# S3 from A11 and A21, two small products exchanged, sums of w_in stored on SP, and one set of q loads earlier, in a fused attention and feed-forward kernel

## The chip, the cores and the metric

The kernel runs on one core of a Trainium2 chip. The engines of the core work beside each other, each through its own instructions in program order: TensorE (PE) multiplies, VectorE (DVE) adds, subtracts and transposes, ScalarE (ACT) squares and copies, GpSimd (POOL) and SyncE (SP) issue transfers. The metric is the time of one execution on the device in microseconds (us), as the median of several; profiles come from one further execution.

## The reference

All tensors are float32. q, k and v have shape (8 batches, 8 heads, 576 rows, 64).

```
kv  = einsum("bhsd,bhse->bhde", k, v)
out = einsum("bhsd,bhde->bhse", q, kv)
x   = out / sqrt(mean(out*out, axis=-1) + 1e-6) * g_norm     # per head
x   = transpose(x, (0, 2, 1, 3)).reshape(4608, 512)
h   = x @ w_in                       # 512 x 2048
g   = s * relu(h)**2 + b
out = g @ w_out                      # 2048 x 512
```

The attention is small. Nearly all arithmetic is in the two products with w_in and w_out.

## The kernel before

The 4608 tokens are cut into nine units of 512, u = 0 to 8. For each, `mm1` computes h and the squared ReLU, and `mm2` computes the product with w_out. Both use Winograd's form of Strassen's scheme: a product of 2 by 2 blocks is made of seven block products instead of eight, for which sums of blocks are formed first: S1 = A21 + A22, S2 = S1 − A11, S3 = A11 − A21, S4 = A12 − S2 on the left, and T1 to T4 in the same way on the right. The seven products have the numbers 1 to 7 in the code: 1 is A11·B11, 2 is A12·B21, 3 is S4·B22, 4 is A22·T4, 5 is S1·T1, 6 is S2·T2, 7 is S3·T3.

Units 0 and 1 go one level deep. Units 2 to 8 are called deep here. In `mm1_deep`, products 2, 3 and 4 are split once more (`small(i, pair, *ms)`, with m the number of the inner product), in the order listed in `DEEP`. In `mm2`, function `rest()` does the same by groups of products: 1, then 2 and 5 together, 6, then 7 and 3 together, then 4. The line of nearly every matmul is that of a helper, L92; additions are L260, subtractions L263, and the fused addition with ReLU L267.

**The four slices of A.** The left operand of mm2, g, lies in tiles ga[name, s] for s = 0 to 3 with names a11, a12, a21, a22 and s1. VectorE writes S2 into the tile of A11, S4 into that of A12, and S3 into that of A21, each in its turn (`s1`, `s2`, `s3`, `s4`, one 128x512 instruction per slice). Before the change S3 is formed as A22 − S2, which is the same value, so it can only come once S2 stands in A11's tile; the four steps come in `rest()` right after S4, between `go_6(7)` and `do_6(5)`. ScalarE makes the square of each A block and applies s and b in `done(name, *slices)` (L944, L651).

**Sums and their buffers.** The sums of weights and of x for the inner products are made by VectorE in buffers with the tag "sub", of which there are six: `sums_of_w_in` (two parts for each of the five keys in `DEEP`), `parts_of_w` (sums of w_out; three with this tag, one with another), `sums_of_x`, `sums_of_x4`, and the quarter sums of mm2. A buffer is free once its last reader is done; for sums of weights that is the transfer that stores them to DRAM. `sums_of_w_in` is made in unit 1 and stored at L794 by POOL into `w1_dram`; `parts_of_w` is made in unit 1's mm2 and stored at L1143 by POOL into `w3_dram`.

**The ring.** From unit 1 on, weights and stored sums come from DRAM through a ring of 14 slots of 256 KB. SP issues the loads in the order of use (`queue_w2`); `used()` frees slots and `pump()` issues the next loads.

**The order of work.** The order on every engine is the order of the program: it is written out by hand in `run()` (mm1 of a deep unit, with `at(n)` for side work), in `rest()` (mm2) and in the tables of `sides()` and `side_of()`. The attention of a later unit is side work: `loads` (q, by `load_q`, L1653, 16 transfers of 32 KB on POOL for one half unit), `turn` (L540, transposes of q on VectorE), `product` (L552, TensorE), `back` (L564), `square`, `row_sum`, `norm`, `turn_x` and `scale`. Output stores (L1246) are on POOL too, until the last unit.

In unit 1, POOL's order around the change is as follows. In mm1: q loads, among which stand the ten stores of `sums_of_w_in`. In mm2: four stores of sums for key 5, four output stores, four stores for key 3, eight output stores, four stores for key 4, four output stores, and then sixteen q loads, `loads(3, 1)`, at step 13 of `side_of`.

Of the kernel before, what the change touches and what calls it, by code (L numbers as in the profile page):

```python
# [17 lines left out]
def kernel(  # L18
# [39 lines left out]
    nc = tc.nc  # L58
# [13 lines left out]
    NS = FC // 4  # L72
# [189 lines left out]
    def sub(o, a, b):  # L262
        nc.vector.tensor_tensor(out=o, in0=a, in1=b, op=ALU.subtract)  # L263
# [47 lines left out]

    w2_dram = [dram.tile([P, 2, FC // 2, P], FP32, name=f"w2_{i}") for i in range(8)]
    w3_dram = [dram.tile([P, 4, FC // 4, P], FP32, name=f"w3_{i}") for i in range(8)]
    DEEP = ((2, 0), (4, 0), (3, 0), (2, 1), (3, 1))
    w1_dram = {key: dram.tile([P, 2, 4 * P], FP32, name=f"w1_{key[0]}{key[1]}") for key in DEEP}
    w_up = convp.tile([P, FC // 2, DM], FP32, name="w_up")
    w_dn = convp.tile([P, FC // 2, DM], FP32, name="w_dn")
# [317 lines left out]
    ga, g_pair = {}, {}  # L635
# [143 lines left out]
    def sums_of_w_in(key):  # L779

        i, pair = key
        w = [
            ws[s][:, 2] if i == 3 else (wa if i == 2 else wb)[s][:, KH:]
            for s in (2 * pair, 2 * pair + 1)
        ]
        a11, a12, a21, a22 = w[0][:, 0], w[0][:, 1], w[1][:, 0], w[1][:, 1]
        t = {}

        def part(n, *steps):
            x = late["sub"].tile([P, FC // 4, P], FP32, name="sub", tag="sub", bufs=6)  # L790
            t[n] = x[:, :2], x[:, 2:]
            for step in steps:
                step()
            nc.gpsimd.dma_start(  # L794
                out=w1_dram[key][:, n], in_=x.rearrange("p f n -> p (f n)")
            )

        return (
            lambda: part(
                0,  # L800
                lambda: sub(t[0][1], a11, a21),
                lambda: sub(t[0][0], a22, t[0][1]),
            ),
            lambda: part(
                1,
                lambda: add(t[1][0], a21, a22),
                lambda: sub(t[1][1], a12, t[0][0]),
            ),
        )

    def mm1_deep(u):
# [54 lines left out]
        def a22(s):  # L866
            t = g_tile("a22", s)
            add_relu(t, st["y", s], ga["a21", s])
# [8 lines left out]
            g_s1(s)  # L877

        def s3(s):
            sub(ga["a21", s], ga["a22", s], ga["a11", s])  # L880

        def small(i, pair, *ms):
            name = {2: "a11", 3: "a21", 4: "a12"}[i]
            g = (i, pair)
            apart = g == (3, 0)

            def to(j, h):
                return g_pair[name, pair][:, j, :, h * P : h * P + P]

            def w_of(m):  # L890
                s0, s1 = 2 * pair, 2 * pair + 1
                raw = {1: (s0, 0), 2: (s0, 1), 4: (s1, 1)}
                if m in raw:
                    s, k = raw[m]
                    return ws[s][:, 2, k] if i == 3 else (wa if i == 2 else wb)[s][:, KH + k]
                n, k = {6: (6, 0), 7: (6, 1), 5: (5, 0), 3: (5, 1)}[m]
                return ring[u, g, n][:, k]

            def bank_for(m):
                if apart:  # L900
                    ps = ps_t.tile([P, 2, 2 * P], FP32, name="st_ps", tag="t")
                    return ps[:, 0].rearrange("p (b c) -> p b c", c=P)
                if m == 1:
                    ps = ps_a.tile([P, DM], FP32, name="sx_ps", tag="x")
                    return ps.rearrange("p (b c) -> p b c", c=P)[:, :2]
                ps = bank_of(("s", m), "z", 1).rearrange("p b (m c) -> p (b m) c", c=P)
                return ps[:, :2]

            def keep(n, j, h):
                tag = f"q{n}" if apart else {1: "r14", 2: "r2_2", 4: "q4"}[n]  # L910
                if apart:
                    tag += "t"
                st[g, n] = late["tmp"].tile([P, 2, P], FP32, name="r", tag=tag)
                add(st[g, n], st[g, "x"], to(j, h))

            for m in ms:
                first = m in (1, 2, 7)
                if first:
                    st[g, "x" if m == 1 else "y"] = bank_for(m)
                ps = st[g, "x" if m in (1, 6, 5, 3) else "y"]  # L920
                w, x = w_of(m), a[i, m]
                for b in range(2):
                    matmul(ps[:, b], w[:, b], x, first and b == 0, True)
                if m == 7:
                    used((u, g, 6))
                elif m == 3:
                    used((u, g, 5))
                if m == 1:
                    keep(1, 0, 0)
                elif m == 2:  # L930
                    add_relu(to(0, 0), ps, st[g, 1])
                elif m == 6:
                    keep(2, 1, 0)
                elif m == 5:
                    keep(4, 1, 1)
                    add_relu(to(1, 1), st[g, "y"], st[g, 4])
                elif m == 3:
                    add_relu(to(0, 1), ps, to(0, 1))
                elif m == 4:
                    add_relu(to(1, 0), ps, st[g, 2])  # L940

        def done(name, *steps):
            for s in steps:
                nc.scalar.square(ga[name, s], ga[name, s])  # L944
                affine(ga[name, s])

        def run(at, early):
            x1(0)
            at(2)
            x1(1)  # L950
            sums_of_x()
            small(2, 0, 1, 2)
            x6(0)
            at(4)
            at(5)
            small(2, 0, 6, 7)
            y7(0)
            at(6)
            small(2, 0, 5)
            a12(0)  # L960
            x6(1)
            at(7)
            small(2, 0, 3, 4)
            y7(1)
            sums_of_x4()
            a12(1)
            x5(0)
            small(4, 0, 1, 2)
            a22(0)
            done("a11", 0, 1)  # L970
            at(8)
            x5(1)
            small(4, 0, 6, 7)
            at(9)
            a22(1)
            done("a22", 0)
            at(10)
            x1(2)
            at(11)
            small(4, 0, 5)  # L980
            x1(3)
            at(12)
            small(4, 0, 3, 4)
            done("a22", 1)
            x6(2)
            at(13)
            small(3, 0, 1, 2)
            y7(2)
            done("a12", 0, 1)
            at(14)  # L990
            small(3, 0, 6, 7)
            small(2, 1, 1, 2)
            x6(3)
            at(15)
            small(3, 0, 5)
            small(2, 1, 6, 7)
            x5(2)
            small(3, 0, 3, 4)
            small(2, 1, 5)
            a22(2)  # L1000
            y7(3)
            done("a21", 0, 1)
            small(2, 1, 3, 4)
            at(16)
            x5(3)
            done("a22", 2)
            s1(0)
            s1(1)
            done("a11", 2, 3)
            a22(3)  # L1010
            early()
            at(18)
            y4(2)
            done("a22", 3)
            small(3, 1, 1, 2)
            done("a12", 2)
            y4(3)
            small(3, 1, 6, 7)
            done("a12", 3)

        def rest_of_3():
# [2 lines left out]

        last = dict(
            p3_5=lambda: small(3, 1, 5), p3_34=rest_of_3,
            s1=lambda: (s1(2), s1(3)), s3=lambda: [s3(s) for s in range(NS)],
        )
        return run, last

# [70 lines left out]
    def mm2(u, step=None, side={}):  # L1101
# [301 lines left out]
        def rest():  # L1403
# [18 lines left out]
            do_1(4)  # L1422
            do_25(2)
            at(1)
            s2((0,))
            do_25(6)
            s2((1,))
# [16 lines left out]
            do_6(2, 6)  # L1444
            s4((1, 2, 3))
            go_6(7)
            step["s3"]()
            do_6(5)
            sums_73((5, 6), 7)
            sums_73((), 3)  # L1450
# [175 lines left out]
    def side_of(A, B, sums, u):  # L1626

        if u == 0:
            return {
                6: [A["turn"], lambda: kv_product(1)],  # L1630
                8: [A["product"], A["back"], A["square"]],
                9: [A["row_sum"], B["turn"]],
                10: [A["norm"], partial(loads, 2, 0), A["turn_x"], A["scale"], B["product"], B["back"], B["square"]],
                11: [B["row_sum"], B["norm"]],
                12: [B["turn_x"], B["scale"], lambda: [fn() for fn in sums_w_in(0)]],
                13: [sums],
            }
        return {
            0: [A["scale"]],
            1: [B["turn"]],  # L1640
            4: [B["product"], B["back"], B["square"]],
            5: [B["row_sum"]],
            6: [B["norm"]],
            8: [B["turn_x"], B["scale"]],
            11: [sums],
            13: [partial(loads, 3, 1)],
        }

    def loads(u, i):
# [131 lines left out]
    for u in range(U):  # L1781
# [16 lines left out]
        for s in range(NS if u > 0 else 0):  # L1798
            a = steps[s]

            def at(n):
                for fn in first.get((s, n), []):
                    fn()
# [75 lines left out]
```

## Time and profile before

| | us |
|---|---|
| median of three executions | 919.71 (919.36 to 922.05) |
| the profiled execution | 921.89 |
| its span in the profile | 920.1 |

| engine | busy us | share |
|---|---|---|
| PE | 897.6 | 98% |
| DVE | 684.2 | 74% |
| ACT | 345.2 | 38% |
| POOL | 266.6 | 29% |

A line of the timeline has the start and length in us, the engine, the line in the kernel, the operation, what is written and read by the program's names, its size, and the number of instructions put together. In brackets stand the idle time of the engine just before it and what ended that. A line of the waits names the engine, what waited, what it waited for, and then the total in us, the times, and the longest. In the page's list of groups the busy time comes first and then the mean length of one in ns.

### The profile page before, as it was taken

What the parts mean: (1) busy time and instruction counts of PE and PEld (TensorE: products, weight loads), DVE (VectorE), ACT (ScalarE), POOL (GpSimd) and SP (SyncE); (2) the same over time, 40 slices, a digit from 0 to 9 for tenths busy, and PEclk for the clock granted to TensorE, in tenths of its full rate; (3) what the DMA queues carried; (4) which work ended last, traced back from release to release, by engine and by line L of the source; (5) the groups of instructions that cost most, each with busy time, mean ns of one, the idle gap of its engine ahead of it and who ended that gap; (6) DMA issues with size and microseconds to landing.
All of it is one profiled execution on the core that took longest, in us unless ns stands there. A gap on an engine that the chain in (4) does not pass through costs nothing.

```text
span 920.1 us, 19738 instructions
## 1 busy us (share of the span) xinstructions
PE 897.6 (98%) x7662; PEld 827.2 (90%) x7662; DVE 684.2 (74%) x1321; ACT 345.2 (38%) x584; POOL 266.6 (29%) x503
## 2 busy tenths in 40 slices
PE   7999999999999999999999999999999999999998
PEld 6888888888879998999899989999999989999998
DVE  2898687785467977688768876887769786974686
ACT  3887024422157005620464026601660066104610
POOL 2037066223721334701570037303520300021000
PEclk9999999999999999999999999999999999999999
DMA  9898647459833985388636973587539812982185
GB/s 255 315 320 244 172 121 252 146 151 350 298 102 108 310 291 159 87 285 287 192 95 212 292 258 77 170 291 264 135 112 293 276 47 65 299 293 66 60 277 180
DMA packets 121166, 188.77 MB, mean 205 GB/s; under 512 B 25457, under 2 KB 43249, under 8 KB 121073
## 3 DMA queue, kind: packets, MB, share of 16 engines
q1 hardware_dynamic: 100304, 159.03, 54.2%
q0 software_dynamic: 17312, 26.25, 9.5%
q10 hardware_dynamic: 3456, 2.23, 1.0%
q8 instruction: 61, 1.00, 0.4%
q14 instruction: 33, 0.26, 0.1%
HBM read 160.70 MB, written 26.74 MB: 204 GB/s over the span
## 4 chain that ended last, share of the span: by engine, by line
PE 81%; DVE 13%; DMA 4%; ACT 1%; issue 1%; ACTq 0%; DVEq 0%; SPq 0%; POOLq 0%
PE x_ps L92 39%; PE y_ps L92 22%; PE z_ps L92 8%; PE sx_ps L92 5%; DVE a L263 4%; PE st_ps L92 2%; DVE sub L263 2%; DVE o L260 2%; PE y_ps L552 2%; DMA w_sb<-w 1%; DVE sub L260 1%; DMA kv_sb<-in_v_dram 1%; DVE r L260 1%; PE kv_ps L384 1%; PE z_ps L384 1%
## 5 line engine op out<-in xcount | busy, mean ns | idle before, releaser
L1653 POOL DMA_DIRECT2D q_sb<-in_q_dram x312 | 175.4, 570 | 120.2 <-issue 61.6
L1246 POOL DMA_DIRECT2D out_dram<-o x120 | 59.4, 502 | 341.5 <-issue 174.5
L92 PE MATMUL x_ps<-w_sb,sub 128*128 128x128 f32 x1176 | 149.2, 276 | 0.1
L92 PEld LDWEIGHTS x_ps<-w_sb,sub 128*128 128x128 f32 x1176 | 139.7, 192 | 0.3 <-DVE r L260 0.2
L651 ACT ACTIVATE a<-a,b_col,s_col 128x512 f32<-128x512 f32 x144 | 117.0, 814 | 27.8 <-DVE a L654 19.5
L848 ACT COPY a<-x_ps 128x512 f32<-128x512 f32 x28 | 16.3, 582 | 246.7 <-PE x_ps L92 246.6
L92 PE MATMUL y_ps<-xs,wb 128*128 128x256 f32 x416 | 98.5, 380 | 0.0
L92 PE MATMUL x_ps<-xs,ws_raw 128*128 128x256 f32 x384 | 91.2, 380 | 1.3 <-ACT r L725 1.3
L92 PE MATMUL x_ps<-xT,wa 128*128 128x256 f32 x360 | 85.8, 387 | 0.1
L92 PEld LDWEIGHTS y_ps<-xs,wb 128*128 128x128 f32 x416 | 76.3, 190 | 9.1 <-issue 0.2
L92 PEld LDWEIGHTS x_ps<-xs,ws_raw 128*128 128x128 f32 x384 | 70.0, 190 | 10.3 <-ACT r L725 2.1
L92 PEld LDWEIGHTS x_ps<-xT,wa 128*128 128x128 f32 x360 | 67.6, 193 | 11.1 <-ACT a L944 1.3
L92 PE MATMUL x_ps<-w_sb,a 128*128 128x128 f32 (+1 forms) x432 | 66.4, 301 | 7.6 <-issue 7.6
L944 ACT ACTIVATE a<-a 128x512 f32<-128x512 f32 x112 | 69.5, 621 | 5.5 <-DVE a L267 5.5
L92 PEld LDWEIGHTS x_ps<-w_sb,a 128*128 128x128 f32 x432 | 58.9, 191 | 12.1 <-issue 9.1
L260 DVE TENSOR_TENSOR r<-sx_ps,a 128x256 f32<-128x256 f32 x84 | 35.0, 417 | 41.3 <-PE sx_ps L92 40.9
L92 PE MATMUL y_ps<-w_sb,a 128*128 128x128 f32 (+1 forms) x416 | 62.1, 295 | 0.0
L92 PEld LDWEIGHTS y_ps<-w_sb,a 128*128 128x128 f32 x416 | 56.1, 192 | 2.1
L260 DVE TENSOR_TENSOR r<-x_ps,o 128x256 f32<-128x256 f32 (+1 forms) x84 | 29.6, 352 | 31.9 <-PE x_ps L92 29.4
L92 PE MATMUL y_ps<-w_sb,sub 128*128 128x128 f32 x392 | 50.2, 277 | 1.4 <-DVE sub L263 1.4
L92 PEld LDWEIGHTS y_ps<-w_sb,sub 128*128 128x128 f32 x392 | 46.5, 192 | 2.7 <-DVE sub L263 2.7
L92 PE MATMUL z_ps<-w_sb,a 128*128 128x128 f32 (+1 forms) x352 | 46.9, 280 | 0.0
(228 smaller groups left out, 1595.0 us busy)
## 6 DMA issues: line engine op xcount, KB each, us to landing
w_sb<-w SPq DMA_DIRECT2D x413, 256.0 KB, 4.6
w<-sub POOLq DMA_DIRECT2D x38, 256.0 KB, 4.9
w_sb<-w SPq DMA_DIRECT2D x14, 512.0 KB, 8.7
out_dram<-o POOLq DMA_DIRECT2D x112, 64.0 KB, 4.0
w_sb<-in_k_dram SPq DMA_DIRECT2D x24, 288.0 KB, 4.2
w_sb<-in_v_dram SPq DMA_DIRECT2D x24, 288.0 KB, 4.4
w_raw<-in_moe_w_in_dram SPq DMA_DIRECT2D x6, 1024.0 KB, 8.0
q_sb<-in_q_dram POOLq DMA_DIRECT2D x160, 32.0 KB, 3.4
```

What stands on the lines that cost most here:

```text
L92: nc.tensor.matmul(o, lhsT=lhsT, rhs=rhs, start=start, stop=stop, skip_group_check=True)
L260: nc.vector.tensor_tensor(out=o, in0=a, in1=b, op=ALU.add)
L263: nc.vector.tensor_tensor(out=o, in0=a, in1=b, op=ALU.subtract)
L384: nc.tensor.matmul(ps[r][(r ^ l) * HB : (r ^ l) * HB + HB, i, :], lhsT=kv[l][0][rows, j, :], rhs=kv[l][1][rows, j, :], start=(j == 0), sto ...
L552: nc.tensor.matmul(ps[l][32 * p : 32 * p + 32, r, lo:hi], lhsT=bd_kv[b % 2][rows, p, at : at + 32], rhs=st["qT"][rows, p, lo:hi], start=Tr ...
L651: nc.scalar.activation(t, t, AF.Identity, scale=s_col, bias=b_col)
L848: nc.scalar.copy(g_tile("a11", s), st["x", s])
L944: nc.scalar.square(ga[name, s], ga[name, s])
L1246: queues[s % 2].dma_start(out=view[b, jj, :, cols], in_=st[name, j][s * w : s * w + w, cols])
L1653: load()
```

## The change

It has four parts.

1. S3 is computed as A11 − A21, in place in A21's tile, and therefore before S2 overwrites A11. Slices 0 and 1 move into `run()`, slices 2 and 3 into `rest()` ahead of the first S2. S1 of slices 0 and 1 also moves to earlier places in `run()`.
2. In `run()`, the small products of S4·B22 (key (3, 0)) and of A22·T4 (key (4, 0)) exchange places, with the keys in `DEEP`, the squares of A21 and A12 (`done`), and the choice of which of the two uses banks of its own (`apart`). `sums_of_x4` and A22 of slice 1 move as well.
3. The ten stores of `sums_of_w_in` are issued by SP instead of POOL.
4. `loads(3, 1)`, q for the second half of the unit with u = 3, is issued at step 9 of unit 1's mm2 instead of step 13: on POOL it now stands behind the stores of key 5 and ahead of the output stores that follow them.

No matmul, addition or activation is added or removed.

```diff
-    DEEP = ((2, 0), (4, 0), (3, 0), (2, 1), (3, 1))
+    DEEP = ((2, 0), (3, 0), (4, 0), (2, 1), (3, 1))
...
-            nc.gpsimd.dma_start(
+            nc.sync.dma_start(
                 out=w1_dram[key][:, n], in_=x.rearrange("p f n -> p (f n)")
             )
...
         def s3(s):
-            sub(ga["a21", s], ga["a22", s], ga["a11", s])
+            sub(ga["a21", s], ga["a11", s], ga["a21", s])
...
-            apart = g == (3, 0)
+            apart = g == (4, 0)
...
             small(2, 0, 3, 4)
             y7(1)
-            sums_of_x4()
             a12(1)
             x5(0)
-            small(4, 0, 1, 2)
             a22(0)
+            small(3, 0, 1, 2)
             done("a11", 0, 1)
             at(8)
             x5(1)
-            small(4, 0, 6, 7)
+            a22(1)
+            small(3, 0, 6, 7)
             at(9)
-            a22(1)
             done("a22", 0)
             at(10)
             x1(2)
             at(11)
-            small(4, 0, 5)
+            small(3, 0, 5)
             x1(3)
             at(12)
-            small(4, 0, 3, 4)
+            small(3, 0, 3, 4)
             done("a22", 1)
+            sums_of_x4()
             x6(2)
             at(13)
-            small(3, 0, 1, 2)
+            small(4, 0, 1, 2)
             y7(2)
-            done("a12", 0, 1)
+            done("a21", 0, 1)
             at(14)
-            small(3, 0, 6, 7)
+            small(4, 0, 6, 7)
             small(2, 1, 1, 2)
             x6(3)
+            s1(0)
             at(15)
-            small(3, 0, 5)
+            small(4, 0, 5)
             small(2, 1, 6, 7)
+            s1(1)
             x5(2)
-            small(3, 0, 3, 4)
+            small(4, 0, 3, 4)
             small(2, 1, 5)
             a22(2)
             y7(3)
-            done("a21", 0, 1)
+            s3(0)
+            done("a12", 0, 1)
             small(2, 1, 3, 4)
             at(16)
             x5(3)
             done("a22", 2)
-            s1(0)
-            s1(1)
+            s3(1)
...
-            s1=lambda: (s1(2), s1(3)), s3=lambda: [s3(s) for s in range(NS)],
+            s1=lambda: (s1(2), s1(3)), s3=lambda: (s3(2), s3(3)),
...
             at(1)
+            step["s3"]()
             s2((0,))
...
             go_6(7)
-            step["s3"]()
             do_6(5)
...
-            13: [partial(loads, 3, 1)],
+            9: [partial(loads, 3, 1)],
```

## The prediction

> **What bounds the kernel now.** I read the page first: busy times and the chain that ended last.
>
> ```profile
> span 920.1 us, 19738 instructions
> PE 897.6 (98%) x7662; PEld 827.2 (90%) x7662; DVE 684.2 (74%) x1321; ACT 345.2 (38%) x584; POOL 266.6 (29%) x503
> PE 81%; DVE 13%; DMA 4%; ACT 1%; issue 1%; ACTq 0%; DVEq 0%; SPq 0%; POOLq 0%
> ```
>
> TensorE is the bound: it stands idle for 920.1 − 897.6 = 22.5 us. The change keeps every matmul, so it can win only where PE waits or runs slowly. TensorE's waits name those places:
>
> ```profile
> PE x_ps L92 <- issue: 7.6, 7, 1.3
> PE y_ps L552 <- DVE qT L540: 2.2, 1, 2.2
> PE y_ps L92 <- DVE sub L263: 1.4, 7, 0.2
> PE x_ps L92 <- ACT r L725: 1.3, 1, 1.3
> ```
>
> Two waits occur seven times, once in each deep unit; two occur once. The timeline of PE and then of DVE, 606 to 622 us (seventh unit), shows the sevenfold ones:
>
> ```profile
> 607.56 1.06 PE L92 MATMUL x_ps<-w_sb,sub 128*128 128x128 f32 x8
> 609.66 2.16 PE L92 MATMUL x_ps<-w_sb,a 128*128 128x128 f32 x16 [1.05 <-issue]
> 615.30 1.95 PE L92 MATMUL x_ps<-w_sb,sub 128*128 128x128 f32 x16
> 617.45 2.05 PE L92 MATMUL y_ps<-w_sb,sub 128*128 128x128 f32 x16 [0.20 <-DVE sub L263]
> ```
>
> ```profile
> 607.08 4.29 DVE L263 TENSOR_TENSOR a<-a,a 128x512 f32<-128x512 f32 x7
> 611.81 0.68 DVE L260 TENSOR_TENSOR sub<-a,a 128x512 f32<-128x512 f32 x1
> 616.71 1.28 DVE L263 TENSOR_TENSOR sub<-a 128x512 f32<-128x512 f32 x2
> ```
>
> The run of seven is S4 of slices 1 to 3 and then S3 of all four. DVE is in order, so the reads of PE's banks and the sums for group (7,3) queue behind it. "issue" is the profile's word where it sees no releaser; the block of seven starts before the gap and ends after it, so I put the gap down to it. Single waits, timelines of DVE and PE in unit 1:
>
> ```profile
> 165.51 0.43 DVE L263 TENSOR_TENSOR sub<-wa,wa 128x256 f32<-128x256 f32 x1 [2.63 <-DMA w<-sub]
> ```
>
> ```profile
> 169.09 1.99 PE L92 MATMUL x_ps<-xs,ws_raw 128*128 128x256 f32 x8 [1.28 <-ACT r L725]
> ```
>
> And where unit 1 gives way to unit 2, timelines of DVE, PE and POOL:
>
> ```profile
> 236.58 0.41 DVE L263 TENSOR_TENSOR sub<-xT 128x256 f32<-128x256 f32 x1
> 259.69 1.25 DVE L540 STREAM_TRANSPOSE qT<-q_sb 128x1024 f32<-128x1024 f32 x1 [1.13 <-DMA q_sb<-in_q_dram]
> ```
>
> ```profile
> 242.11 0.61 PE L92 MATMUL sx_ps<-sub,w_sb 128*128 128x128 f32 x4
> 260.99 1.10 PE L552 MATMUL y_ps<-qT,bd_kv 64*32 64x256 f32 x32 [2.20 <-DVE qT L540]
> 262.02 3.68 PE L92 MATMUL x_ps<-xT,wa 128*128 128x256 f32 x8
> ```
>
> ```profile
> 228.50 2.31 POOL L1143 DMA_DIRECT2D w<-sub  x4
> 252.56 0.58 POOL L1653 DMA_DIRECT2D q_sb<-in_q_dram  x1 [1.69 <-DMA q_sb<-in_q_dram]
> ```
>
> DVE waits for q and PE for DVE. The eight matmuls after it take 3.68 us where their form takes 1.89 elsewhere: half clock.
>
> **What the Trainium skill says.** "Perfetto Trace Analysis", Tensor Engine Instruction: "ACT/DVE/GPSIMD are strict FIFO". The trace agrees: one DVE wait of 2.63 us holds every later DVE step. "TensorE: Matmul & The Clock Gate", What's actually happening: an idle window of about 3.4 us, free-running, puts TensorE on half clock. Here slow matmuls follow the 2.20 us gap, for about 3.4 us (262.1 to 265.5), and none follow the gaps of 1.05 to 1.3; so a gap of 2 us is already a risk. "DMA: Bandwidth & Descriptors", Issuing engines are not separate DMA queues: transfers of SP and POOL interleave on the same 16 DMA engines. So moving stores to SP frees POOL's order and semaphores, not bandwidth; the trace before has no such store on SP to test this.
>
> **The change, part by part.** No instruction is added or removed on PE, DVE or ACT.
>
> *S3 out of the stretch before (7,3).* PE's loss there now, by starts against the steady 0.1117 us a matmul (16 in 1.787): the block due at 607.56 + 0.893 = 608.45 starts at 609.66 (1.21 late); the blocks to 615.30 lose 0.28 more; the one due at 617.09 starts at 617.45 (0.36); the next loses 0.09. Sum 1.94 us. The fifth unit's same stretch gives 1.92. After: four subtractions at 0.60 apart, 2.4 us, leave the block. S4 of slice 1 is what the late block needs and comes first anyway; the sums for (7,3) come 2.4 us earlier, 0.6 us before PE wants them. Both waits should go.
>
> Where the four land: S3 of slices 2 and 3 (1.2 us) go ahead of S2 of slice 0, where DVE idles 0.30 and 0.69 us within 4 us; the read of PE's bank behind them ends near 500.5, needed at 501.0, a margin of 0.5. S3 of slices 0 and 1 and the earlier S1 of 0 and 1 (0.6 to 0.68 each) fall among DVE waits for small products of 1.64, 1.85 and 0.69 us in the fifth unit. Covered, so nothing; without the cover 2.4 us a unit. The new S3 needs A11 and A21, which ScalarE squares; A21's slices 0 and 1 should be through near 469.8, wanted at 471.1: margin 1.3.
>
> Six units at 1.94 make 11.6. In unit 2 the norm and transposes of a second attention share DVE's front, and I take half, 1.0. Gain 12.6; bounds 6 (DVE still full there) to 14 (some of the small waits in front go too).
>
> *Exchange of the small products of S4·B22 and A22·T4, with what moves beside them.* The same matmul shapes in the same sequence. Which sums are wanted when shifts by one group; the margins I find are 0.25 to 0.7 us. Taken as 0; bounds −1 to +4 over seven units.
>
> *Stores of w_in's sums on SP.* Ten stores of 256 KB. Now they stand on POOL behind up to 48 q loads (0.57 us each), and DVE waits for one to release its buffer. On SP they go out when the sum is ready, and land before 154, when the buffer is wanted near 163. The 2.63 us on DVE goes, and with it the late start of PE: due at 167.65 (165.92 plus 1.73), seen at 169.09, 1.44. Gain 1.5 with its tail; bounds 0 to 2. On SP they are queued between weight loads; a late sum or a full ring there holds stores and loads, but the later stores' readers come only from 184 on. Taken as hidden; if the loads were held, the ring's lead, 13 slots of eight matmuls (0.893 us) or 11.6 us, against a load's 4.6, would have to be used up first.
>
> *q of the fourth unit at step 9, not 13.* It lands near 240 instead of 259.6. The transpose cannot start before DVE is through with the previous product's (257.26 + 1.30), so PE's product starts near 259.85, not 260.99: 1.14. A gap of 1.06 us should spare the half clock: 1.7 of its 3.4 us. Gain 2.85; bounds 1.1 to 2.85.
>
> *What that pushes back.* On POOL the sixteen loads, 9.3 us to issue with landing waits between, now stand after w_5's four stores and ahead of the output stores and w_3's four stores. The latter went out at 228.50; they will at about 236 to 238. They hold buffers of "sub" (six) that DVE's sums of x want at 236.58. Landing after issue was about 4.9 us, so DVE gets its buffers at 240.9 to 243.1 (1.5 earlier in the new frame): a DVE wait of 4 to 7. PE has other matmuls until 242.11, then needs those sums through: late by 1.6 to 6, I take 3.5. After such a gap half clock is likely (chance 0.65 of 1.7, 1.1). Cost 4.6; bounds 0 (POOL gets through faster) to 8.
>
> Sum: −12.6 − 1.5 − 2.85 + 4.6 = −12.3. The profiled execution took 921.89 us with a span of 920.1; its median is 919.71. Span 907.8; median about 907.5.
>
> DMA as the next bound: its engines were busy 0.91 in 505.5 to 521.7, so PE cannot win there without loads in hand; but the ring's 11.6 us against landings of up to 7.5 there outlasts a gain of 1.9.
>
> **Rivals.**
> - *No stall at the sums of x.* POOL's q loads go faster than I think, or the buffers are free. For: the page has q landing 3.4 us after issue. Against: the order on POOL. 919.7 − 12.6 − 1.5 − 2.85 = 902.8, say 903.
> - *DVE stays the limit before (7,3).* DVE was busy 15.36 of 16.20 us in 505.5 to 521.7; other sums there may still be late, and only half of S3's 12.6 comes: 907.5 + 6.3 ≈ 913.5. Against: 2.4 us of those 15.36 leave.
> - *It does nothing*: the waits move to the place where S3 is now made and cost as much there. 919 to 920.
> - *Slower: the new S1 or S3 waits for ScalarE's square of A21.* On the in-order DVE that wait stands ahead of the reads of the small products' banks, in each of seven units. Margin 1.3 us, then 1.64 of DVE idle. It decides when the squares come 1.3 + 1.64 + 2.2 = 5.1 us late: then 2.2 × 7 = 15 us outweigh 12.3 and leave 3 more. With 3 us a unit: 907.5 + 21 = 928.5. For: the margins are hand-made. Against: ACT is busy only 38%.
>
> **How the numbers follow.** Likeliest, 907.5 (905 to 910.5): 0.44. No stall, 903: 0.18. Half the S3 gain, 913.5: 0.18. Nothing: 0.06. Slower: 0.14. Within 0.3% (2.8 us), a measurement can't tell from no change. Range 901.5 to 916: the first three cases, 0.80, with the bounds of the stall (−4.6, the 903 case) and of S3 in it. Faster 0.80, same 0.06, slower 0.14.
>
> **What will show it.** Right: no PE wait "issue" or "DVE sub" in the (7,3) stretch of the deep units; no DVE wait for a w_in store near 165; the transpose of q without its DMA wait, and the following x_ps at 1.89; a new DVE wait for the store of w at the sums of x, and PE late after it. Wrong: the seven waits under another name, DVE waiting on ACT ahead of S1, or ring loads as PE's releaser. The forecast falls most if S3's new place is not free.

## The result and the profile after

The changed kernel takes 909.53 us (median of four, 907.86 to 909.94) against 919.54 (919.28 to 922.05). The ratio is 0.988 with an interval of 0.986 to 0.990, so it is faster by 10.0 us, or 1.1%. The profiled execution took 909.79 us, with a span of 908.0.

The page of the changed kernel, span, busy times and chain:

```profile
span 908.0 us, 19742 instructions
PE 892.4 (98%) x7662; PEld 825.4 (91%) x7662; DVE 683.4 (75%) x1321; ACT 345.5 (38%) x584; POOL 261.5 (29%) x493
PE 83%; DVE 6%; issue 4%; DMA 3%; POOL 2%; ACT 1%; SPq 0%; DVEq 0%; POOLq 0%
```

DVE's share of the chain falls from 13% to 6%. PE's busy time falls by 5 us although it runs the same 7662 matmuls; part of the delay lay inside blocks that count as busy (2.16 us, before, for a block of sixteen that takes 1.95). PE's waits after, those that concern the change:

```profile
PE sx_ps L92 <- DVE r L260: 3.3, 1, 3.3
PE y_ps L552 <- DVE qT L540: 1.1, 1, 1.1
PE x_ps L92 <- DVE r L260: 1.0, 1, 1.0
```

The two sevenfold waits are gone, and so is the one for ACT in unit 1. The wait for q's transpose is half as long. Two waits are new at the places of the change, 3.3 and 1.0 us, each once.

Where the time went can be read matmul by matmul, since PE runs the same matmuls in the same order: I took the start of each in both traces and noted where the difference changes. Slow matmuls start about twice as far apart as the same ones elsewhere: 0.43 us for 0.21 in the eight of `x_ps<-xT,wa` after q's product.

| place (start before) | what changes | us |
|---|---|---|
| 169.09 | the wait for a store in unit 1 | −1.53 |
| 242.11 | the new wait at the sums of x | +3.32 |
| 242.3 to 243.9 | slow matmuls after it | +1.76 |
| 260.99 | q's transpose | −1.08 |
| 262.6 to 265.5 | slow matmuls after it, gone | −1.68 |
| 305.19 | new wait in unit 2 | +1.20 |
| 316.94, 324.73 | the pair of waits, unit 2 | −2.08 |
| the same pair, six units | 1.95 each, with drift between | −11.79 |
| sum | | −11.88 |

The span falls by 12.1; the other 0.2 lies behind the last matmul.

PE and then DVE in the fifth unit's stretch before group (7,3), timelines of the changed kernel. The stretch shown of before is the seventh unit's; by PE's starts the fifth lost the same there.

```profile
507.66 1.06 PE L92 MATMUL x_ps<-w_sb,sub 128*128 128x128 f32 x8
508.55 1.95 PE L92 MATMUL x_ps<-w_sb,a 128*128 128x128 f32 x16
513.91 1.95 PE L92 MATMUL x_ps<-w_sb,sub 128*128 128x128 f32 x16
515.70 1.95 PE L92 MATMUL y_ps<-w_sb,sub 128*128 128x128 f32 x16
```

```profile
507.18 1.89 DVE L263 TENSOR_TENSOR a<-a,a 128x512 f32<-128x512 f32 x3
509.51 0.68 DVE L260 TENSOR_TENSOR sub<-a,a 128x512 f32<-128x512 f32 x1
```

The run of seven subtractions is a run of three, and PE's blocks follow each other at 0.89 and 1.79 us without a gap.

Unit 1 and its passage to unit 2, timelines of PE, DVE and POOL after:

```profile
167.56 1.89 PE L92 MATMUL x_ps<-xs,ws_raw 128*128 128x256 f32 x8
...
243.90 1.22 PE L92 MATMUL sx_ps<-sub,w_sb 128*128 128x128 f32 x4 [3.26 <-DVE r L260]
...
263.47 1.10 PE L552 MATMUL y_ps<-qT,bd_kv 64*32 64x256 f32 x32 [1.13 <-DVE qT L540]
264.50 2.00 PE L92 MATMUL x_ps<-xT,wa 128*128 128x256 f32 x8
```

```profile
240.19 0.42 DVE L263 TENSOR_TENSOR sub<-xT 128x256 f32<-128x256 f32 x1 [5.15 <-DMA w<-sub]
...
242.75 0.42 DVE L263 TENSOR_TENSOR sub<-xT 128x256 f32<-128x256 f32 x1 [1.68 <-DMA w<-sub]
```

```profile
222.03 2.91 POOL L1655 DMA_DIRECT2D q_sb<-in_q_dram  x5
...
236.29 2.17 POOL L1145 DMA_DIRECT2D w<-sub  x4
```

The store of key 3's sums moved from 228.50 to 236.29, behind the q loads. DVE's first sum of x waits 5.15 us for its buffer, and PE waits 3.26 us for DVE. The four matmuls that follow take 1.22 us instead of 0.61.

### The profile page after: what moved, and what is told of

Same layout as the page of the kernel before. It is cut to its first block, busy times and chain, and to the rows that moved or that the text cites. A ratio compares the mean times of both kernels' runs of the same rounds, so it can differ in the third digit from the quotient of the medians.

```text
span 908.0 us, 19742 instructions
## 1 busy us (share of the span) xinstructions
PE 892.4 (98%) x7662; PEld 825.4 (91%) x7662; DVE 683.4 (75%) x1321; ACT 345.5 (38%) x584; POOL 261.5 (29%) x493
## 4 chain that ended last, share of the span: by engine, by line
PE 83%; DVE 6%; issue 4%; DMA 3%; POOL 2%; ACT 1%; SPq 0%; DVEq 0%; POOLq 0%
PE x_ps L92 40%; PE y_ps L92 22%; PE z_ps L92 10%; PE sx_ps L92 6%; PE st_ps L92 2%; PE y_ps L552 2%; DMA w<-sub 1%; POOL w L1145 1%; DMA kv_sb<-in_v_dram 1%; DMA q_sb<-in_q_dram 1%; PE kv_ps L384 1%; DVE sub L263 1%; PE z_ps L384 1%; DVE a L263 1%; POOL q_sb L1655 1%
## 5 line engine op out<-in xcount | busy, mean ns | idle before, releaser
L260 DVE TENSOR_TENSOR r<-sx_ps,a 128x256 f32<-128x256 f32 x84 | 35.1, 418 | 26.2 <-PE sx_ps L92 25.7
L260 DVE TENSOR_TENSOR r<-x_ps,o 128x256 f32<-128x256 f32 (+1 forms) x84 | 29.7, 353 | 27.7 <-PE x_ps L92 27.0
L263 DVE TENSOR_TENSOR a<-a,a 128x512 f32<-128x512 f32 x72 | 46.7, 684 | 0.1
```

Source lines behind the costliest of these rows:

```text
L260: nc.vector.tensor_tensor(out=o, in0=a, in1=b, op=ALU.add)
```

## The experiments

Two theories stood to begin with. The account: the parts add up as in the table, with S3's place worth 12.7 us and the q move a net loss, because POOL's order delays a store. The rivals: the push-back is due to traffic or to the stores on SP; and S3's gain is due to the exchange of the small products.

**q back at step 13.**

```diff
-            9: [partial(loads, 3, 1)],
+            13: [partial(loads, 3, 1)],
```

> The changed kernel with the q loads back at step 13. Account of the two traces: S3 and its order are worth -12.7 us, the stores on SP -1.5, q earlier -2.8, and POOL's delayed stores +5.1. So without the q move the span should be 920.1 - 12.7 - 1.5 = 905.9 (2.1 below the changed kernel), no DVE wait for a store at the sums of x, and PE's wait of about 2.2 us for q's transpose back, with slow matmuls after it. Rival, that the stall at the sums of x comes from the stores on SP or from denser traffic and not from POOL's order: the stall of about 5 stays and the span is 910 to 911.

Span 905.3, median 905.4; ratio to the kernel before 0.984 (0.981 to 0.986). There is no DVE wait for a store, and PE's wait for the transpose is back at 1.84 us. Slow matmuls follow that wait, as before. So the changed kernel carries a part that costs it some 4 us in the medians, 2.7 in the spans. The stores on SP do not stall the sums of x.

**q at step 10.**

```diff
-            9: [partial(loads, 3, 1)],
+            10: [partial(loads, 3, 1)],
```

> The changed kernel with the q loads at step 10, behind the stores of key 3 on POOL and ahead of those of key 4. If POOL's order is what stalls the sums of x, both go: no wait of 5 us on DVE, and q still lands before the product before it is through (PE waits 1.1, no slow matmuls). Span 920.1 - 12.7 - 1.5 - 2.8 = 903.1. Rival, that the earlier q as such is what delays the stores: about 908, as the changed kernel. Second rival, that q now comes too late: 905 to 906, as with step 13.

Span 903.2, median 904.6; ratio 0.982 (0.980 to 0.985). POOL's and then DVE's timeline in this kernel:

```profile
227.14 1.63 POOL L1145 DMA_DIRECT2D w<-sub  x3
229.12 0.54 POOL L1145 DMA_DIRECT2D w<-sub  x1 [0.34 <-DVE xs L263]
229.65 1.77 POOL L1655 DMA_DIRECT2D q_sb<-in_q_dram  x3
```

```profile
235.22 0.41 DVE L263 TENSOR_TENSOR sub<-xT 128x256 f32<-128x256 f32 x1
```

The stores of key 3 are out ahead of q, the first sum of x starts without a wait, and q still comes in time. The same sixteen loads one place later give both gains. It is POOL's order that stalls.

**Its opposite test: q at step 9, on SP.**

```diff
-            9: [partial(loads, 3, 1)],
+            9: [lambda: [load() for load in load_q(14, rest_on=nc.sync)]],
```

> The changed kernel with its sixteen q loads at step 9 issued by SP instead of POOL. If what stalls the sums of x is POOL's order, the stores of key 3 go out near 227 again and the 5 us wait goes, though the same bytes move at the same time: span near 903, as with step 10. If it is traffic on the DMA engines, the wait stays and the span is near 908. A third possibility: sixteen issues on SP hold up the loads of the ring, and PE waits for a ring load in mm2 of unit 1.

Span 905.3, median 906.6; ratio 0.986 (0.984 to 0.987). The sums of x start at 234.98 with no wait, so it is not the traffic. Yet the span is 2.1 us above that of step 10. SP's queue and PE in this kernel, and the line on L114 from the view of that line:

```profile
222.06 10.85 SPq L1648 DMA_DIRECT2D q_sb<-in_q_dram  x16
233.03 0.42 SPq L114 DMA_DIRECT2D w_sb<-in_k_dram  x1
233.55 0.42 SPq L114 DMA_DIRECT2D w_sb<-in_v_dram  x1
```

```profile
DMA to landing us min/median/max: 5.0/5.1/5.2
```

```profile
243.63 1.96 PE L384 MATMUL kv_ps<-w_sb 64*64 64x64 f32 x117
247.31 0.68 PE L384 MATMUL kv_ps<-w_sb 64*64 64x64 f32 x27 [1.72 <-issue]
```

The issues hold SP for 10.85 us, and the last loads of k and v stand behind them. PE waits 1.72 us within the product of k and v, and by PE's starts that gap is the 2.0 us that this kernel loses to step 10. It looks like the third possibility, but the loads are not its cause: they landed 5.0 and 5.2 us after issue, at 238.1 and 238.8, before the product began at 243.63. The trace names no releaser. It has a transfer of the kind "instruction" from 244.8 to 245.8, where the gap begins (245.6 to 247.3); in the step-10 kernel the like one was over by 240.6. Whether PE stood without instructions was not tested, and the cause stays open.

**q at step 9 alone, on the kernel before.**

```diff
-            13: [partial(loads, 3, 1)],
+            9: [partial(loads, 3, 1)],
```

> The q loads at step 9 alone, on the kernel before. If the pushed-back stores cost what they cost in the changed kernel, the span is 920.1 - 2.8 + 5.1 = 922.4, slower than before, with a DVE wait of 5 us or more for the store ahead of the sums of x. Rival, that the push-back came only together with the other parts: 917.3, faster.

Median 923.5 against 919.9, ratio 1.0035 (1.0027 to 1.0044): slower. Waits of DVE and the timeline of PE in this kernel:

```profile
DVE sub L263 <- DMA w<-sub: 9.6, 3, 5.2
```

```profile
245.48 0.71 PE L92 MATMUL sx_ps<-sub,w_sb 128*128 128x128 f32 x4 [3.23 <-DVE r L260]
246.04 0.71 PE L92 MATMUL z_ps<-sub,w_sb 128*128 128x128 f32 x4
246.59 1.89 PE L92 MATMUL y_ps<-xs,wb 128*128 128x256 f32 x8
```

The stall comes with the q move alone; the third of these waits is the one in unit 1, which this kernel keeps. The span of its profile, 920.8, is below the 922.4 expected because the matmuls after the 3.23 us wait run at full speed here, which they did not in the changed kernel.

**S3 and the exchange alone** (parts 1 and 2; from the changed kernel).

```diff
-            nc.sync.dma_start(
+            nc.gpsimd.dma_start(
                 out=w1_dram[key][:, n], in_=x.rearrange("p f n -> p (f n)")
...
-            9: [partial(loads, 3, 1)],
+            13: [partial(loads, 3, 1)],
```

> Parts 1 and 2 alone (S3 from A11 and A21 in its new places, and the exchanged small products). Account of the traces: span 920.1 - 12.7 = 907.4; unit 1 as before with PE's waits of 1.3 and 2.2 us; the seven pairs of waits gone; in unit 2 a wait of about 1 us for a read of VectorE stays. Rival, that the gain needs the other parts (stores off POOL): over 909.

Span 906.2, median 908.4; ratio 0.987 (0.984 to 0.989). By PE's starts the deep units give −12.7 us, as in the changed kernel; the rest against 907.4 is that no slow matmuls followed its wait for q, though that wait was longer, 2.67 us, than the 2.2 expected. S3 needs no help from the other parts.

**S3's new place without the exchange,** on the kernel before. All four slices go ahead of the first S2; `s1` and the small products stay as before.

```diff
-            sub(ga["a21", s], ga["a22", s], ga["a11", s])
+            sub(ga["a21", s], ga["a11", s], ga["a21", s])
...
             at(1)
+            step["s3"]()
             s2((0,))
...
             go_6(7)
-            step["s3"]()
             do_6(5)
```

> The kernel before with S3 from A11 and A21, all four slices ahead of the first S2, and the order of the small products, S1 and everything else as before. It tells the new place of S3 from the exchange around it. The seven pairs of waits before group (7,3) should go as in the changed kernel (1.95 us a unit); but four subtractions, not two, stand ahead of the read of PE's bank, whose margin in the changed kernel's fifth unit is 0.5 us: 1.2 us more make PE late by about 0.7 in each of six units and by 1.2 more in unit 2. Gain 12.7 - 4.2 - 1.2 = 7.3, span 912.8. Rival, that the exchange is not needed at all: 907. Second rival, that the gain is that of the exchange: 918 or more.

Span 914.0, median 915.4; ratio 0.995 (0.993 to 0.997). Its waits of PE, and DVE in the fifth unit:

```profile
PE x_ps L92 <- DVE r L260: 7.1, 7, 2.2
```

```profile
496.37 2.49 DVE L263 TENSOR_TENSOR a<-a,a 128x512 f32<-128x512 f32 x4
498.78 0.68 DVE L263 TENSOR_TENSOR a<-s,a 128x512 f32<-128x512 f32 x1
499.38 0.42 DVE L260 TENSOR_TENSOR r<-x_ps,o 128x256 f32<-128x256 f32 x1
```

The waits before (7,3) go, and in each deep unit one for the read at L260 comes, which stands behind the four subtractions: PE's starts fall back by 0.87 us per unit in six, 0.16 more soon after, and by 2.40 in unit 2. I had put 0.7 and 2.4. So the place is not free for four slices; for two it is free in six units, while unit 2 pays 1.20. By PE's starts the deep units give 4.7 us here, not the 7.3 expected and not the 12.7 of the changed kernel; the rest of the lower span is that no slow matmuls followed the wait for q.

**The exchange without S3's new place** (from the kernel above with parts 1 and 2).

```diff
-            sub(ga["a21", s], ga["a11", s], ga["a21", s])
+            sub(ga["a21", s], ga["a22", s], ga["a11", s])
...
-            s3(0)
...
-            s3(1)
...
-            s1=lambda: (s1(2), s1(3)), s3=lambda: (s3(2), s3(3)),
+            s1=lambda: (s1(2), s1(3)), s3=lambda: [s3(s) for s in range(NS)],
...
-            step["s3"]()
             s2((0,))
...
             go_6(7)
+            step["s3"]()
             do_6(5)
```

> Part 2 alone: the exchanged small products with S1 in its earlier places, while S3 stays A22 - S2 and in its old place. If the gain of parts 1 and 2 is that of S3's place, and the exchange only makes room for two of its slices, the seven pairs of waits of 1.05 and 0.20 us stay and the span stays at 920 (918.4 where the slow matmuls after q's wait don't come). Rival, that the earlier S1 and the exchange take load off the stretch on their own: 914 to 917.

Span 919.3, median 920.4; ratio 0.9994 (0.998 to 1.0007). Its waits of PE:

```profile
PE x_ps L92 <- issue: 7.6, 7, 1.3
PE y_ps L92 <- DVE sub L263: 1.4, 7, 0.2
```

Both sevenfold waits are there in full. The exchange, with S1 in its earlier places, gives nothing by itself. That it makes room for S3's slices 0 and 1 in `run()` is read from the order of the code (A21 must be squared before them): no kernel here puts them there without it.

**Stores of w_in's sums on SP alone**, on the kernel before.

```diff
-            nc.gpsimd.dma_start(
+            nc.sync.dma_start(
                 out=w1_dram[key][:, n], in_=x.rearrange("p f n -> p (f n)")
```

> The stores of the sums of w_in on SP alone, on the kernel before. Account: the DVE wait of 2.6 us for a store near 165 goes and the matmuls due at 167.65 start there instead of 169.09: 1.5 us, span 918.6 where the slow matmuls after q's wait stay as they were, 916.9 where they don't come. Rival, that the gain is eaten by the wait for q that follows (the q loads stay where they are, behind the same queue): PE's wait for the transpose grows from 2.2 to 3.7 and the span stays 920.

Median 919.18 against 919.49, ratio 0.9993 (0.998 to 1.0005): nothing to be told in the times. In the trace PE's starts come 1.49 us earlier from 169.09 on and stay so until the matmuls after q's product; those are not slow here, and the span is 916.7. Compared at the same granted clock of TensorE, the executions differ too: at 0.999 to 1.000 they average 918.1 (six) against 919.7 (twelve), at 0.998 or below 920.5 (six) against 921.7 (two). So a gain of 1.2 to 1.5 us is there, and the difference between the clocks, some 2 us, hides it. The sorting by clock was made after the result, and six of twelve lie at the lower clock against two of fourteen: whether stores on SP make that clock more frequent is not shown. PE in this kernel's trace:

```profile
259.38 1.10 PE L552 MATMUL y_ps<-qT,bd_kv 64*32 64x256 f32 x32 [2.18 <-DVE qT L540]
260.41 1.99 PE L92 MATMUL x_ps<-xT,wa 128*128 128x256 f32 x8
```

Before, the same eight matmuls after the same wait (2.20 us) took 3.68 us.

**The changed kernel once more,** with no edit.

> The changed kernel once more, unaltered, for how often TensorE's granted clock falls below 0.999 in it. If the half clock after a wait depends on where the wait falls and not on its length alone, executions at 1.000 and at 0.998 both occur, about 2 us apart, with the 3.3 us wait in each; the median then lies between 907.5 and 909.8. If the wait of 3.3 us brings half clock each time, all executions are at 0.998 and near 909.8.

Median 909.42. Three of four executions at 0.997 or 0.998 took 909.2 to 909.8, one at 1.000 took 907.0. With the first four that makes six of eight at the lower clock. Its trace has a wait of 2.86 us at the sums of x, with slow matmuls after it. The half clock is frequent, not certain.

**q at step 10, and unit 2's second norm moved** (from the kernel with q at step 10).

```diff
             done("a11", 2, 3)
+            at(17)
             a22(3)
...
                 15: [B["row_sum"]],
                 16: [A["scale"]],
+                17: [B["norm"]],
             }
-            second = {1: [B["norm"]], 2: [B["turn_x"]], 3: [*q[1]], "sums": [B["scale"]]}
+            second = {2: [B["turn_x"]], 3: [*q[1]], "sums": [B["scale"]]}
```

It aims at the new 1.03 us wait of unit 2. In the changed kernel, DVE and PE there:

```profile
303.76 1.22 DVE L585 TENSOR_TENSOR xn<-q_sb,inv 128x1024 f32<-128x1024 f32 x1
304.90 1.28 DVE L263 TENSOR_TENSOR a<-a,a 128x512 f32<-128x512 f32 x2
306.11 0.68 DVE L263 TENSOR_TENSOR a<-s,a 128x512 f32<-128x512 f32 x1
306.71 0.42 DVE L260 TENSOR_TENSOR r<-x_ps,o 128x256 f32<-128x256 f32 x1
```

```profile
307.18 2.05 PE L92 MATMUL x_ps<-w_sb,sub 128*128 128x128 f32 x16 [1.03 <-DVE r L260]
```

> The kernel with q at step 10, and in unit 2 the second norm (1.5 us on VectorE) moved ahead of A22 of slice 3, where VectorE idles 1.32 us for ScalarE. In unit 2 the norm and the two S3 together are ahead of the read that PE waits 1.03 us for; if the norm is what makes that read late there, and not in the other units, the wait goes and the span falls by 1.2 from 903.2 to 902. Rival, that VectorE is full throughout unit 2's mm2 whatever stands there: the wait shows up later by as much and the span stays 903.

Span 901.5, median 903.4 (903.24 to 903.53); ratio 0.982 (0.981 to 0.984). PE's wait is gone and nothing takes its place: the sum of the norm and two S3 ahead of that read was the cause. At 903.4 against 909.5 this kernel beats both.

## Why the prediction was right, by its steps

The span forecast was 907.8 and is 908.0; the median forecast was 907.5 and is 909.53, inside the range.

*S3 out of the stretch: 12.6 forecast, 12.7 measured.* In each of six units 1.94 was summed from late starts, and 1.95 came: a sum that holds whatever the late block waits for. What it waits for I had read wrongly. The block is `go_73(1)`, the first inner products of S3·T3 and S4·B22, and the code takes S3 first; I had named S4 of slice 1. S3 of slice 0 is the fourth in the run of seven. DVE's timeline of before, 608.99 to 609.4:

```profile
608.88 0.68 DVE L263 TENSOR_TENSOR a<-a,a 128x512 f32<-128x512 f32 x1
```

It ends at 609.56, and PE starts at 609.66. In all seven deep units of the kernel before, the block's first matmul starts 0.10 us after the fourth subtraction ends, and its fifth matmul 0.06 us after the next one, S3 of slice 1, ends. So behind the gap that the page calls "issue" stands S3 itself, made too late, and not a queue of reads; only the second wait, 0.20 us for a sum, is of that kind. Taking S3 out of the run removed both.

*Unit 2: right in size, wrong in place.* I took half of 1.94 because DVE's front would be full there. The pair of waits went in full, 2.08; 1.20 came back at the read behind the norm and two S3, which I had not named. Net 0.88 for 1.0.

*The places where the four slices land: covered, as said,* with the margin of 0.5 us that S3 of slices 2 and 3 had: two slices more made PE late by 0.87 in S3's place alone, where 1.2 − 0.5 = 0.7 was to be expected.

*Exchange: 0 forecast.* With it alone PE's starts move by 0.06 us over all seven deep units, and the ratio is 0.9994.

*Stores on SP: 1.5 forecast,* 1.53 and 1.49 measured by PE's starts.

*q earlier: 2.85 forecast,* 1.08 + 1.68 = 2.76 measured, in part by luck. The 1.08 is the shorter wait. The 1.68 is the slow block after it, which the profiled execution of before had and others need not have: with the stores alone, S3 alone and S3's place alone q still came late, and none followed. The medians of step 10 and step 13 differ by 0.8 us, not by 2.8.

*What that pushes back: 4.6 forecast, 5.1 measured.* DVE was to wait 4 to 7 and waited 6.8 in two pieces; PE was to be 3.5 late and was 3.3; the term that was mis-sized is the half clock, 1.1 as a chance, 1.76 as it fell. The q move as a whole therefore costs more than it brings, and a place one step later is free of that cost.

*The rivals.* No stall did not happen, though the step-10 kernel shows that most of it was to be had: a median of 904.6 where the rival said 903. DVE as the limit before (7,3) did not hold: PE's records there have no gap at all after. The wait for ScalarE's square ahead of S1 or S3 did not occur. DVE does wait more for ScalarE's copies (L861), 24.8 us in 21 waits for 7.1 in 13, ahead of A22; PE does not wait for it in turn.

*From span to median: the step that failed.* I let the median stand as far from the profiled execution as before, that is 2.2 us below. Of the kernel before, that execution was one at the lower clock, 921.89 with a median of 919.5; of the changed kernel, 909.79 lies beside its median, because six of its eight executions are at the lower clock. So the change gives 11.9 us in the two traces and 10.0 in the medians. At equal clock it gives more: beside the second measurement of the changed kernel, the kernel before averages 919.6 at 0.999 or 1.000 (eight) and 922.3 below (seven), against 907.0 (one) and 909.5 (three) of the changed kernel: 12.6 and 12.7 us, at the price of few executions. That the stall at the sums of x makes the slow block frequent is supported by q at step 9 alone: 14 of 20 executions are below 0.999, against 6 of 23 of the kernel before beside it. It is not the only cause, since S3's place alone, without the stall, has three of four there.

## What to carry to other kernels

On an engine that runs in order, find the instructions that stand in the busiest stretch and ask when their inputs were ready: an algebraically equal form with earlier inputs (A11 − A21 for A22 − S2) can move them to where the engine idles, as far as the margin there goes, which was two slices and not four. Ask first which single instruction the late block takes its input from, and compare the end of it with the block's start in every repetition: a gap without a named releaser then gets one. A transfer asked for sooner is put ahead of others on its queue; look for who holds a buffer until one of those has landed, and move it one place past them. Compare PE's starts matmul by matmul when its work is unchanged: gains of 1.5 us that the times hide are then plain. And before a loss seen in one trace is counted as a gain, see whether the other executions have it.

## What was not expected of the hardware

The half clock after a wait does not go by the wait's length. PE in S3's place alone:

```profile
261.27 1.10 PE L552 MATMUL y_ps<-qT,bd_kv 64*32 64x256 f32 x32 [2.20 <-DVE qT L540]
262.30 1.99 PE L92 MATMUL x_ps<-xT,wa 128*128 128x256 f32 x8
```

The kernel before has the same wait of 2.20 us, and its eight matmuls took 3.68. After waits for q's transpose of 2.20, 1.97 and 1.84 us (kernel before, exchange alone, step 13) slow matmuls followed; after 2.20, 2.18 and 2.67 us (S3's place alone, stores alone, S3 alone) none did. At the sums of x they were slow after 3.26 and 2.86 us (changed kernel, twice), and not after 3.23 us (q alone). After the waits of 0.95 to 1.13 us for the transpose, in six traces, none followed. "TensorE: Matmul & The Clock Gate" of the Trainium skill, What's actually happening, puts the slow state after at least one idle window of about 3.4 us and says that the window runs freely, so that the point of change at a kernel's start depends on where in the window the first matmul lands. Here waits of 1.84 to 3.26 us were enough, all shorter than that figure. If a wait's place in the window counts in the same way within a kernel, pairs of equal length and different outcome would follow; no run here varied that place by itself, so it is not shown.

One such block costs about 1.7 us, which is 0.2% of the span. In the traces that have one at these places the granted clock of the whole execution is 0.998, in those without it 0.999 or 1.000. Times of other executions do not all sort by that clock: S3's place alone took 914.2 to 915.7 us at 0.997 or 0.998 and 915.8 at 0.999. The kernel without long waits in this part (step 10 with the norm moved) spread over only 0.3 us.
